# Mid and last chunks of a spectral mix: y of two more chunks spread by TensorE instead of by DMA, and three pieces of TensorE work moved

## The chip, the cores and the metric

The kernel runs on one core of a Trainium2 chip. The metric is the device time of one execution in microseconds (us). Times without a unit are us from the start of the profiled span.

## What is computed

The program is a causal attention with a cumulative bias, followed by a mix in the frequency domain:

```python
# q, k, v: (8, 8, 576, 64); s: (8, 8, 576); w_r, w_i: (64, 512, 512); w_ch: (512, 512)
scores = q @ k^T / sqrt(64) + min(-(cum[i] - cum[j]), 0), causal
x = softmax(scores) @ v                        # as (8, 576, 512)
X = rfft(x, axis=1)                            # along the sequence
Yr = Xr*w_r - Xi*w_i ; Yi = Xr*w_i + Xi*w_r    # 64 modes, each its own 512x512 pair
y = irfft(Y padded with zeros, n=576)
u = x + y
out = u + max(u @ w_ch, 0)                     # (8, 576, 512), float32
```

## The kernel before, in words

**Stages.** Attention goes over 32 steps (four groups g of two heads, eight batches b each). Its result x stays on chip as `x_all`. Per step a small product with sines and cosines gives the 64 modes of x, kept in `xs`. Group by group, the modes are multiplied by their weights: `modes(g, c)` (L430) takes chunk c of eight modes, with four weight tiles x = 0 to 3 (real and imaginary part, even and odd modes) of 512 KB each, and sixteen matmuls of 32 columns, four side by side in the column groups of the array. Groups 0 to 2 add up in `y_acc`; the last group's result plus `y_acc` goes to `yb` (L455, VectorE), which is Y of chunk c with 128 rows: four mode pairs, real and imaginary part, and batch.

**Weights.** 128 weight tiles, 64 MB in the type they have on chip, are streamed by GpSimd's queue (L217) into a ring of eleven slots (`wpool`) for the last 52 of them. A tile's transfer is issued when the matmuls that read the slot's former tile are done.

**The order of the work** is written out by hand (`manual_schedule`): each engine runs its instructions in program order, and waits on semaphores only for its data and for the release of tiles. The part that matters here is the loop over the eight chunks of the last group (L757 to L790) and what it calls:

- The final result of a row block is relu((x + y) Wch) + x + y. A "pair" is two row blocks of 128; there are 18. For 16 of them x Wch is made early and kept: six during attention, ten ("late") in this loop. `work()` (L673) does one step of that: `x_transposed` (L586: eight matmuls with the identity, two VectorE copies L596) of the next pair, and `keep` (L607) of the pair before: eight matmuls (L602), then ScalarE's copy (L492); for pairs of way "e" ScalarE's copy (L494) and VectorE's residual (L495). The calls go around the chunk loop by `TAKE` (L687) and by `gather`'s `turns`. The two first pairs' products, `x_times_wch(0)` and `(1)`, stay in PSUM.
- To add y, the inverse transform needs Y with modes on the partitions: tile `yv`, partition 16c + (8 modes, two parts), with batch, "which" (0 for y, 1 for v = y Wch) and 512 columns behind it. There are two ways to it. `spread` (L464) is a DMA transfer on SP's queue of 128 KB from `yb` or `vb` to `yv`. `gather` (L641) reads `yt_first`, kept transposes of y of several chunks, and picks one batch's columns as the stationary side; 64 columns at a time (two batches side by side) it makes v (moving side Wch, L653) and y (moving side the identity), and ScalarE (L665) and VectorE (L663) copy each to `yv`.
- Chunks 0 to 3: `y_transposed` (L622: four transposes, ScalarE's copy L627) into `yt_first`; after chunk 3, `gather(0, 4, 3)`: four blocks of v and y, with `work()` after the first three.
- Chunks 4 and 5: `modes` (it spreads y), `y_transposed` into a small tile, `y_times_wch` (L630: four matmuls L633, VectorE's copy L637, spread of v). After them the last `work()`, `x_transposed(0)`, `x_times_wch(0)`.
- Chunk 6: the same with the two first pairs' work between; chunk 7: `modes` with the first pairs' sums between its weight tiles (`first_u` ahead of x = 2, `first_z` ahead of x = 3). Y of chunks 6 and 7 is added straight from `yb` for the first two pairs (`add_last`), and spread for the others.
- Then, for the other pairs, the sums with x, y and the kept products, relu on ScalarE, the final add on VectorE and the output transfers on SP.

**PSUM.** `yp` (modes), `yt_ps`, `v_ps` and `yg_ps` share a ring of two banks, tag "aux" (L106); `xt_ps` a ring of two ("u"), `z_ps` a ring of two ("z").

Of the kernel before, what the change touches and what calls it, by code (L numbers as in the profile page):

```python
# [9 lines left out]
FP32 = mybir.dt.float32  # L10
FP16 = mybir.dt.float16
# [7 lines left out]
def kernel(  # L19
# [14 lines left out]
    DM = H * D  # L34
    P = 128
# [5 lines left out]
    DT = DM // P  # L41
# [5 lines left out]
    NCK = NM // MC  # L47
# [57 lines left out]
    spool = ctx.enter_context(tc.tile_pool(name="small_sb", bufs=2))  # L105
    auxpool = ctx.enter_context(tc.tile_pool(name="aux_psum", bufs=2, space=PSUM))  # L106
# [323 lines left out]
    def modes(g, c, meanwhile=None):  # L430


        ps = auxpool.tile([P, DM], FP32, name="yp", tag="aux")
        for x in range(4):
            ri, par = divmod(x, 2)
            cols = xs[g % 2].rearrange("p k r b m -> p (k r b) m")
            c0 = (48, 16)[ri] - 16 * par
            if meanwhile and x in meanwhile:
                meanwhile[x]()
            for cg in range(4):  # L440
                nc.tensor.matmul(  # L441
                    ps[32 * cg : 32 * cg + 32, :],
                    cols[:, c0 : c0 + 32, c * MC + 2 * cg + par],
                    wt[(g, c, ri, par)][:, cg, :],
                    start=(x == 0), stop=(x == 3),
                    tile_position=(0, 32 * cg), skip_group_check=True,
                )
        if g == 0:
            nc.vector.tensor_copy(out=y_acc[:, c, :], in_=ps)
        elif g < NG - 1:  # L450
            nc.vector.tensor_tensor(out=y_acc[:, c, :], in0=ps, in1=y_acc[:, c, :], op=ALU.add)
        else:
            yb = spool.tile([P, DM], FP16, name="y_sb", tag="y")
            for cols in halves if c == NCK - 1 else [slice(0, DM)]:
                nc.vector.tensor_tensor(  # L455
                    out=yb[:, cols], in0=ps[:, cols], in1=y_acc[:, c, cols], op=ALU.add
                )
            if c >= NCK // 2:
                spread(c, 0, yb)
            return yb  # L460

# [2 lines left out]
    def spread(c, which, rows):  # L464

        nc.sync.dma_start(out=yv[16 * c : 16 * c + 16, :, which, :], in_=rows)
# [113 lines left out]
    def parts(b, T):  # L580

        if T < NF:
            return [(slice(0, P), b, ident16h)]
        return [(slice(NL * i, NL * i + NL), b + i, ident16h[:NL, :NL]) for i in range(2)]

    def x_transposed(i):  # L586
        xts[i] = xt_sb[len(xts) % 2]
        for x, (b, T) in enumerate(pairs[i]):
            ps = upool.tile([P, DT, P], FP32, name="xt_ps", tag="u")
            for rows, bb, ident in parts(b, T):  # L590
                for dt in range(DT):
                    nc.tensor.matmul(
                        ps[:, dt, rows], x_all[: rows.stop - rows.start, dt, bb, T, :],
                        ident, start=True, stop=True, skip_group_check=True,
                    )
            nc.vector.tensor_copy(out=xts[i][:, x], in_=ps)  # L596

    def x_times_wch(i, last):
        zs[i] = z = zpool.tile([P, 2, DM], FP32, name="z_ps", tag="z")
        for x in range(2):  # L600
            for dt in range(DT):
                nc.tensor.matmul(  # L602
                    z[:, x, :], xts[i][:, x, dt, :], wch_sb[:, dt, :],
                    start=(dt == 0), stop=(last and dt == DT - 1), skip_group_check=True,
                )

    def keep(i):  # L607
        x_times_wch(i, True)
        j = late.index(i)
        if j < len(places):  # L610
            t = places[j]
        else:
            t = wpool.tile([P, WM, DM], BF16, name="z1", tag="w").rearrange("p m e -> p (m e)")
        kept_place(i, t)
        keep_product(i, slice(0, 2), zs[i])
# [3 lines left out]
    NY = NCK // 2  # L619
    yt_first = finpool.tile([P, DT, NY, P], FP16, name="yt_first")  # L620

    def y_transposed(yb, c=NCK):  # L622
        ps = auxpool.tile([P, DT, P], FP16, name="yt_ps", tag="aux")
        for dt in range(DT):
            nc.tensor.transpose(ps[:, dt, :], yb[:, bass.ts(dt, P)], ident16h)
        yt = yt_first[:, :, c, :] if c < NY else spool.tile([P, DT, P], FP16, name="yt_sb", tag="yt")
        nc.scalar.copy(out=yt, in_=ps)  # L627
        return yt

    def y_times_wch(c, yt):  # L630
        vp = auxpool.tile([P, DM], FP32, name="v_ps", tag="aux")
        for dt in range(DT):
            nc.tensor.matmul(  # L633
                vp, yt[:, dt, :], wch_sb[:, dt, :], start=(dt == 0), stop=(dt == DT - 1)
            )
        vb = spool.tile([P, DM], FP16, name="v_sb", tag="v")
        nc.vector.tensor_copy(out=vb, in_=vp)  # L637
        spread(c, 1, vb)
        return vb

    def gather(c0, c1, turns):  # L641

        n = 2 * MC * (c1 - c0)
        rows = slice(2 * MC * c0, 2 * MC * c1)
        ng = P // n
        for b0 in range(0, B, ng):
            vp = auxpool.tile([P, DM], FP32, name="v_ps", tag="aux")
            yp = auxpool.tile([P, DM], FP32, name="yg_ps", tag="aux")
            for which, ps in ((1, vp), (0, yp)):
                for dt in range(DT):  # L650
                    for g in range(ng):
                        op = yt_first[:, dt, : c1 - c0].rearrange("p c (x b) -> p (c x) b", b=B)
                        nc.tensor.matmul(  # L653
                            ps[n * g : n * g + n, :] if which else ps[n * g : n * g + n, bass.ts(dt, P)],
                            op[:, :, b0 + g],
                            wch_sb[:, dt, :] if which else ident16h,
                            start=(dt == 0 or not which), stop=(dt == DT - 1 or not which),
                            tile_position=(0, n * g), skip_group_check=True,
                        )
                for g in range(ng):  # L660
                    dst, src = yv[rows, b0 + g, which, :], ps[n * g : n * g + n, :]
                    if g % 2:
                        nc.vector.tensor_copy(out=dst, in_=src)  # L663
                    else:
                        nc.scalar.copy(out=dst, in_=src)  # L665
            if turns:
                turns -= 1
                work()


# [2 lines left out]
    def work():  # L673

        if not order_z and not ahead:
            return
        if order_z:
            i = order_z.pop(0)
            x_transposed(i)
            ahead.append(i)  # L680
        if len(ahead) == 2 or not order_z:
            i = ahead.pop(0)
            keep(i)

    late = [i for i in kept if i not in first_pairs]
    order_z = list(late)
    TAKE = (3, 2, 2, 0, 0, 0)  # L687
    us, rs = {}, {}
    GK = P - 2 * MC * NX

# [66 lines left out]
    for c in range(NCK - 2):  # L757
        yb = modes(NG - 1, c)
        for x in range(TAKE[c] - 1):
            work()  # L760
        yt = y_transposed(yb, c)
        if TAKE[c]:
            work()
        if c >= NY:
            y_times_wch(c, yt)
        elif c == NY - 1:
            gather(0, NY, 3)
    work()
    assert not order_z and not ahead
    c = NCK - 2  # L770
    x_transposed(0)
    x_times_wch(0, False)
    yb6 = modes(NG - 1, c)
    x_transposed(1)
    yt = y_transposed(yb6)
    x_times_wch(1, False)
    vb6 = y_times_wch(c, yt)
# [14 lines left out]
    yt = spool.tile([P, DT, P], FP16, name="yt_sb", tag="yt")  # L792
    for x in range(2):
        dts = slice(x * DT // 2, (x + 1) * DT // 2)
        ps = auxpool.tile([P, DT // 2, P], FP16, name="yt_ps", tag="aux")
# [5 lines left out]
    for cols in halves:  # L801
        vp = auxpool.tile([P, DM // 2], FP32, name="v_ps", tag="aux")
# [81 lines left out]
```

## Time and profile before

| | before |
|---|---|
| median of 6 runs | 458.14 us (456.3 to 458.77) |
| the profiled execution | 458.25 us, span 456.4 us |
| TensorE matmuls | 347.9 us busy (76%), 4201 |
| TensorE weight loads | 220.1 us busy (48%), 4233 |
| VectorE | 238.2 us busy (52%), 531 |
| ScalarE | 219.7 us busy (48%), 386 |
| GpSimd | 183.0 us busy (40%), 269 |
| mean granted TensorE clock | 0.872 |
| DMA | 94.01 MB, 206 GB/s over the span |
| the two spread kinds, `yv<-y_sb` and `yv<-v_sb` | 4 each, 128 KB each, 5.6 and 4.4 us to land (medians) |

How to read it: the page's 40 slices are 11.4 us each; a digit is the busy share in tenths, and for PEclk the clock granted to TensorE. A timeline line has start, duration, engine, line of the kernel, operation, out<-in, partitions and sizes, and how many instructions of that kind follow each other; in square brackets, how long the engine was idle before the first of them and what ended that. PE is TensorE, DVE VectorE, ACT ScalarE, POOL GpSimd, SP the queue of SyncE. The span goes from the first instruction to the last; the execution's time has 1.85 us around it.

### The profile page before, as it was taken

The page shows a single profiled execution, that of the slowest core. Times are in us where ns is not written, and L with a number is a line of the kernel's source. Part 1 is how long each engine was busy: PE and PEld are TensorE (multiplying, and loading weights), DVE is VectorE, ACT ScalarE, POOL GpSimd, SP SyncE. Part 2 cuts the span into 40 slices and gives each one's busy share as a digit, 9 for nine tenths or more (in the row PEclk, how much of TensorE's full clock was granted, in tenths as well). Part 3 has the DMA queues.
Part 4 walks back from the last instruction along what each step waited for, and adds up shares of the span by engine and source line. Part 5 has one row for each costly group of instructions (what it writes and reads, how often), then busy time and mean ns, then how long its engine had stood idle before and what let it go on. Part 6 is the DMA issues. An engine that isn't in the chain of part 4 may idle for free.

```text
span 456.4 us, 10298 instructions
## 1 busy us (share of the span) xinstructions
PE 347.9 (76%) x4201; PEld 220.1 (48%) x4233; DVE 238.2 (52%) x531; ACT 219.7 (48%) x386; POOL 183.0 (40%) x269
## 2 busy tenths in 40 slices
PE   1879888966562978826587778799879769689995
PEld 1456666644342656614455555466545336334432
DVE  7775665653242556614345535455745425532796
ACT  1585886554241657713445345366632224211774
POOL 6755555544345555334454454355423231300000
PEclk9997999997587899967778769799986978779999
DMA  9999999999999999999999999999999999993688
GB/s 178 201 203 203 202 201 204 203 204 204 204 204 201 202 203 203 203 205 204 200 196 204 204 204 205 203 203 202 207 206 208 206 207 206 210 217 76 226 297 318
DMA packets 108799, 94.01 MB, mean 206 GB/s; under 512 B 28416, under 2 KB 103936, under 8 KB 108752
## 3 DMA queue, kind: packets, MB, share of 16 engines
q0 software_dynamic: 98960, 81.81, 113.1%
q1 hardware_dynamic: 9792, 11.55, 8.0%
q8 instruction: 33, 0.54, 0.4%
q14 instruction: 14, 0.11, 0.1%
HBM read 164.56 MB, written 9.44 MB: 381 GB/s over the span
## 4 chain that ended last, share of the span: by engine, by line
DMA 55%; PE 28%; DVE 8%; issue 4%; POOL 2%; ACT 1%; SPq 0%; DVEq 0%; POOLq 0%; ACTq 0%
DMA w_sb<-in_moe_w_r_dram 20%; DMA w_sb<-in_moe_w_i_dram 17%; DMA q<-in_q_dram 13%; DMA k<-in_k_dram 4%; PE sc_ps L365 4%; PE av_ps L394 3%; PE yp L441 3%; PE sc_ps L359 3%; PE tr_ps L324 3%; PE z_ps L695 2%; DVE qtB L327 2%; PE ft_ps L418 2%; PE u_ps L714 1%; DVE qtA L327 1%; PE u_ps L695 1%
## 5 line engine op out<-in xcount | busy, mean ns | idle before, releaser
L373 ACT ACTIVATE p_sb<-sc_ps,cumt_sb 128x576 f16<-128x576 f32 (+1 forms) x256 | 141.9, 635 | 47.6 <-PE sc_ps L365 47.1
L217 POOL DMA_DIRECT2D w_sb<-in_moe_w_i_dram x60 | 45.1, 751 | 86.3 <-PE yp L441 42.0
L217 POOL DMA_DIRECT2D w_sb<-in_moe_w_r_dram x60 | 45.4, 757 | 62.6 <-DMA w_sb<-in_moe_w_r_dram 24.2
L217 POOL DMA_DIRECT2D v<-in_v_dram x72 | 50.8, 707 | 31.0 <-DMA v<-in_v_dram 8.4
L359 PE MATMUL sc_ps<-negm,ident 128*128 128x256 bf16 x256 | 56.4, 307 | 0.2
L324 PE MATMUL tr_ps<-ident,q 64*64 64x64 bf16 x576 | 17.4, 210 | 50.1 <-DMA q<-in_q_dram 50.0
L441 PE MATMUL yp<-w_sb,xs 128*32 128x512 bf16 x480 | 37.2, 417 | 16.7 <-DMA w_sb<-in_moe_w_i_dram 11.7
L327 DVE COPY qtA<-tr_ps 64x576 bf16<-64x576 bf16 x32 | 23.7, 742 | 46.0 <-PE tr_ps L324 46.0
L394 PE MATMUL av_ps<-v,p_sb 128*128 128x65 f16 x1024 | 45.4, 199 | 0.0
L344 ACT ACTIVATE p<-sc_ps,cumt 128x64 f16<-128x64 f32 x32 | 10.0, 313 | 71.5 <-PE sc_ps L340 71.5
L394 PEld LDWEIGHTS <-p_sb 128*128 128x128 f16 x1024 | 40.3, 101 | 5.0 <-issue 1.0
L327 DVE COPY ktA<-tr_ps 64x576 bf16<-64x576 bf16 x32 | 24.0, 749 | 33.0 <-PE tr_ps L324 33.0
L324 PEld LDWEIGHTS <-q 64*64 64x64 bf16 x576 | 13.6, 123 | 52.8 <-DMA q<-in_q_dram 51.7
L365 PE MATMUL sc_ps<-qtB,ktB 128*128 128x64 bf16 (+2 forms) x160 | 35.1, 325 | 3.7 <-issue 2.4
L365 PE MATMUL sc_ps<-qtA,ktA 65*128 65x512 bf16 (+2 forms) x192 | 37.4, 305 | 0.3 <-DVE ktA L327 0.3
L399 DVE TENSOR_REDUCE den<-av_ps 128x5 f32<-128x10 f32 x64 | 10.8, 169 | 51.1 <-PE av_ps L394 51.1
L441 PEld LDWEIGHTS <-xs 128*32 128x32 bf16 x512 | 22.5, 170 | 26.7 <-issue 23.3
L404 DVE TENSOR_TENSOR x_all<-av_ps,rcp 128x320 f16<-128x320 f32 x64 | 31.5, 492 | 2.2
L365 PEld LDWEIGHTS <-ktB 128*128 128x128 bf16 x192 | 22.5, 117 | 15.1 <-issue 6.6
L327 ACT COPY ktB<-tr_ps 64x576 bf16<-64x576 bf16 x32 | 20.3, 633 | 19.5 <-DVE ktA L327 18.5
L602 PE MATMUL z_ps<-wch_sb,xs 128*128 128x512 f16 x96 | 28.0, 444 | 0.8 <-DVE xs L596 0.8
L324 PE MATMUL tr_ps<-ident,k 64*64 64x64 bf16 x576 | 17.6, 211 | 13.8 <-DVE qtB L327 10.1
(117 smaller groups left out, 532.4 us busy)
## 6 DMA issues: line engine op xcount, KB each, us to landing
w_sb<-in_moe_w_r_dram POOLq DMA_DIRECT2D x60, 512.0 KB, 11.9
w_sb<-in_moe_w_i_dram POOLq DMA_DIRECT2D x60, 512.0 KB, 11.9
q<-in_q_dram POOLq DMA_DIRECT2D x32, 144.0 KB, 9.7
k<-in_k_dram POOLq DMA_DIRECT2D x32, 144.0 KB, 10.0
v<-in_v_dram POOLq DMA_DIRECT2D x72, 64.0 KB, 9.7
out_dram<-r_sb SPq DMA_DIRECT2D x16, 256.0 KB, 2.2
out_dram<-r_w SPq DMA_DIRECT2D x16, 256.0 KB, 2.7
x_all<-in_moe_w_i_dram POOLq DMA_DIRECT2D x3, 512.0 KB, 10.1
```

The lines of the kernel that those rows point to most:

```text
L217: nc.gpsimd.dma_start(out=dst, in_=src)
L324: nc.tensor.transpose(ps[rows, r, :], src[rows, r, :], ident16[rows, rows])
L327: copy(out=dst[n % NQ][rows, :].rearrange("d (p r) -> d p r", r=R), in_=ps[rows].rearrange("d r p -> d p r"),)
L359: nc.tensor.matmul(ps[:, bass.ds(w * S, W)], ident16, negm[:, bass.ts(r, W)], start=True, stop=False, skip_group_check=True,)
L365: nc.tensor.matmul(ps[:, c0 : c0 + i1 - i0], keys[:, w, r, :], qt[:, i0:i1], start=False, stop=True, skip_group_check=True,)
L373: nc.scalar.activation(out=pt[:, poff[x] : poff[x] + S - w * W], in_=ps[:, w * S : (w + 1) * S - w * W], func=ACTF.Exp, bias=cumt_sb[:, x, ...
L394: nc.tensor.matmul(ps[:, I, r : r + NCH], lhsT, rhs, start=(i == 0), stop=(i == len(todo) - 1), skip_group_check=True,)
L399: nc.vector.tensor_reduce(out=den, in_=ps[:, :, 0 : VW : NCH], axis=mybir.AxisListType.X, op=ALU.add)
L404: nc.vector.tensor_tensor(out=x_all[:, g, b, :, D * h : D * h + D], in0=ps[:, :, 1 : NCH], in1=rcp.unsqueeze(2).to_broadcast([P, NT, D]), ...
L441: nc.tensor.matmul(ps[32 * cg : 32 * cg + 32, :], cols[:, c0 : c0 + 32, c * MC + 2 * cg + par], wt[(g, c, ri, par)][:, cg, :], start=(x == ...
L602: nc.tensor.matmul(z[:, x, :], xts[i][:, x, dt, :], wch_sb[:, dt, :], start=(dt == 0), stop=(last and dt == DT - 1), skip_group_check=True,)
L695: nc.tensor.matmul(dst[x][r, :], G_sb[rows, bass.ds(T * P, r.stop - r.start)], yv[rows, bb, which, :], start=start, stop=True, skip_group_ ...
```

## The change

Four edits, all in the chunk loop of the last group:

1. y of chunks 4 and 5 is no longer spread by a transfer. Their transposes are kept in `yt_first` (slots 0 and 1, free after the first gather), and after chunk 5 a second `gather` makes y alone from them: 32 columns (two chunks of 16 rows) a matmul, four batches in the four column groups, two blocks of sixteen matmuls, four copies to `yv` a block. v of these chunks is spread as before.
2. `gather` takes a list of kinds, and allocates a bank for each as it comes to it.
3. `work()` in the first gather comes after its second and its fourth block, instead of after its first, second and third. One step of `work()` goes between `y_transposed` and `y_times_wch` of chunk 4, the last step to the same place of chunk 5.
4. `x_transposed(0)` goes between `modes` and `y_transposed` of chunk 5.

The number of the `work()` steps and the order of the pairs are the same.

```diff
-            if c >= NCK // 2:
+            if c >= NCK - 2:
                 spread(c, 0, yb)
...
-        yt = yt_first[:, :, c, :] if c < NY else spool.tile([P, DT, P], FP16, name="yt_sb", tag="yt")
+        yt = yt_first[:, :, c % NY, :] if c < NCK - 2 else spool.tile([P, DT, P], FP16, name="yt_sb", tag="yt")
...
-    def gather(c0, c1, turns):
+    def gather(c0, c1, turns, kinds):
...
-            vp = auxpool.tile([P, DM], FP32, name="v_ps", tag="aux")
-            yp = auxpool.tile([P, DM], FP32, name="yg_ps", tag="aux")
-            for which, ps in ((1, vp), (0, yp)):
+            for which in kinds:
+                ps = auxpool.tile([P, DM], FP32, name="g_ps", tag="aux")
...
-            if turns:
-                turns -= 1
+            if b0 // ng in turns:
                 work()
...
-    TAKE = (3, 2, 2, 0, 0, 0)
+    TAKE = (3, 2, 2, 0, 1, 1)
...
+        if c == NCK - 3:
+            x_transposed(0)
         yt = y_transposed(yb, c)
         if TAKE[c]:
             work()
         if c >= NY:
             y_times_wch(c, yt)
+            if c == NCK - 3:
+                gather(NY, NCK - 2, (), (0,))
         elif c == NY - 1:
-            gather(0, NY, 3)
-    work()
+            gather(0, NY, (1, 3), (1, 0))
     assert not order_z and not ahead
     c = NCK - 2
-    x_transposed(0)
     x_times_wch(0, False)
```

## The prediction

> All times are us of the profiled execution unless marked ns. Chunks are called by the code's c (0 to 7), so "chunks five and six" are c=4 and c=5.
>
> **What bounds the kernel now.** I read the page's slices first, then the chain of waits, the timelines of TensorE, VectorE and ScalarE from 366 to 423, and last busy time by stretches.
>
> ```profile
> PEclk9997999997587899967778769799986978779999
> DMA  9999999999999999999999999999999999993688
> ```
>
> DMA is full for 36 of 40 slices (to 410.7): the weight stream bounds the kernel until TensorE has chunk 3's last tile at 372.88. The diff touches nothing earlier. From there to 421.9 TensorE's own order decides; the stage after it (sixteen pairs of results) is carried by VectorE, 2.5 to 2.9 busy in most 3 us stretches from 432 on, and only shifts. So I follow TensorE to the last weight product (x=3 of c=7), which starts at 418.04. TensorE timeline:
>
> ```profile
> 375.41 1.99 PE L653 MATMUL v_ps<-wch_sb,yt_first 128*64 128x512 f16 x8 [0.67 <-ACT yt_first L627]
> ...
> 381.60 1.14 PE L653 MATMUL v_ps<-wch_sb,yt_first 128*64 128x512 f16 x8
> 382.57 0.58 PE L653 MATMUL yg_ps<-ident16h,yt_first 128*64 128x128 f16 x8
> 383.08 0.62 PE L592 MATMUL xt_ps<-ident16h,x_all 128*128 128x128 f16 x8
> 383.54 1.89 PE L602 MATMUL z_ps<-wch_sb,xs 128*128 128x512 f16 x8
> ...
> 392.27 1.12 PE L441 MATMUL yp<-w_sb,xs 128*32 128x512 bf16 x16 [1.60 <-DMA w_sb<-in_moe_w_r_dram]
> 394.19 0.40 PE L625 MATMUL yt_ps<-ident16h,y_sb 128*128 128x128 f16 x4 [0.80 <-DVE y_sb L455]
> 395.27 1.89 PE L633 MATMUL v_ps<-wch_sb,yt_sb 128*128 128x512 f16 x4 [0.68 <-ACT yt_sb L627]
> ```
>
> TensorE waits 1.60, 0.80 and 0.68 here, the last two again for c=5. The 1.60 is put down to a DMA, wrongly I think: that weight tile was issued at 355.52 and such tiles land 19.8 later. VectorE's timeline names another: the copy that frees the accumulator bank (ring of two, tag "aux") ends at 392.22, late because the residual of an "e" pair (L495) ran first.
>
> ```profile
> 390.27 1.22 DVE L495 TENSOR_TENSOR y_acc<-z_ps,y_acc 128x1024 f16<-128x1024 f32 x1 [0.50 <-ACT y_acc L494]
> 391.53 0.69 DVE L663 CAST yv<-v_ps 64x512 f16<-64x512 f32 x1
> ```
>
> Busy time by stretches (length, then busy and count of TensorE's matmuls, its weight loads, VectorE, ScalarE and GpSimd, then granted clock, DMA share, GB/s):
>
> ```profile
> 391.21:394.62 3.41, 1.52 (x20) 0.91 (x19) 2.28 (x4) 0.15 (x1) 1.48 (x2) 1.00 1.24 206
> 394.62:398.03 3.41, 2.76 (x16) 0.92 (x20) 0.69 (x1) 0.58 (x1) 1.49 (x2) 0.50 1.24 206
> 398.03:401.45 3.42, 1.93 (x17) 0.61 (x10) 0.69 (x1) 0.58 (x1) 0.74 (x1) 0.50 1.22 218
> 401.45:404.86 3.41, 3.41 (x9) 1.22 (x8) 0.69 (x1) 0.00 (x0) 0.00 (x0) 0.50 1.20 230
> 404.86:408.27 3.41, 2.85 (x20) 1.43 (x18) 1.29 (x2) 1.01 (x1) 0.00 (x0) 1.00 1.23 214
> ...
> 336.59:340.01 3.42, 2.02 (x32) 1.40 (x34) 1.45 (x6) 0.59 (x1) 1.25 (x2) 1.00 1.24 207
> ...
> 162.52:165.93 3.41, 1.71 (x30) 1.24 (x31) 1.68 (x3) 0.90 (x4) 1.44 (x2) 1.00 1.33 200
> ...
> 66.94:70.36 3.42, 2.14 (x36) 1.36 (x34) 1.92 (x3) 2.42 (x6) 1.59 (x3) 1.00 1.30 202
> ```
>
> All changes of the granted clock lie on one grid of 3.413. A stretch with 1.52 busy is followed by half clock; after 2.02 (336.59) the clock fell, after 1.71 and 2.14 it did not. From half clock it came back only after stretches at least 3.06 busy. So the waits cost twice: from 394.62 to 404.86 products take double (y times Wch 1.82 start to start against 0.96 at 412.82), some 3.7 in all.
>
> The Trainium skill, "TensorE: Matmul & The Clock Gate", Part 1, has the clock fall only after a whole idle window of about 3.4 us. The row of 391.21 contradicts it. By the rule the two falling-clock rivals below could not happen; by the row they can. The forecast's sum is one and the same.
>
> **The change, walked along TensorE.** Start-to-start costs at full clock: gather's v block 0.97, its y block 0.51, a pair's transposes 0.46, its product 1.82 before a switch to narrow tiles and 1.73 otherwise, the sixteen weight products 1.05 (408.57 to 409.62), transposes of y 0.24, y times Wch 0.96. At half clock: 1.78, 0.58, 0.83 and 427 ns a product matmul.
>
> Gather of c=0 to 3: two blocks now follow each other without a pair between. Block 0 is as before (375.41 to 377.77), but block 1's first bank is free only when ScalarE's and then VectorE's copy is through, 378.05+0.69=378.74: start 378.79, a gap of 1.02. It leaves the stretch from 377.55 with 2.5 busy instead of 3.42, too little to bring the clock back, so I keep half clock to 384.38 (before: 380.97). Block 1 ends 381.15, the pair's transposes 381.98, its product with 5.6 matmuls slow and 2.4 fast 385.0. Block 2 to 386.48; its bank comes free 2.48 after its start (381.60 to 384.08 in the rows), so block 3 starts 387.53, a gap of 1.05; then 389.01, and the second pair ends 391.29. The weight products of c=4 start there, 0.98 earlier, with one pair (2.2) fewer done; the 1.60 wait is gone since a pair now lies between.
>
> c=4: the wait for y_sb stays: 1.92 from the weight products to the transposes gives 393.21. Then the moved pair (2.19) covers the 0.68 wait, y times Wch starts 395.64, c=5's weight products 396.60, x_transposed(0) 397.65 to 398.11. What is late next is VectorE: the moved pair is the "e" one, and its residual now stands before v_sb(4) and y_sb(5). ScalarE L494 starts 1.93 after the product (395.84), VectorE L495 1.04 later (396.88), v_sb 1.26 after that (398.14), y_sb 0.61 on (398.75), the transposes 0.75 on: 399.50, a gap of 1.39 in place of 0.87.
>
> c=5: the last pair covers the 0.68 wait: 401.47; y times Wch to 402.43. Here the new gather comes: 32 matmuls of 32 columns by 128. No row has that form. The nearest are 64 ns each (eight yg_ps in 0.51) and 66 ns each (sixteen weight products in 1.05); four side by side in a quarter of the first would be 16 ns, half clock on the second 132. I take 64, the nearest in width: 2.05. At 16 the copies below would hold c=6 instead, and the sum falls by 1.0; at 132 it rises by 2.2. To 404.47; x_times_wch(0), its 0.56 wait gone, to 406.30.
>
> Evacuation of the new gather: eight copies of 32x512, four to a bank. Rows of 64 and 128 partitions both take VectorE 0.69, so I take 0.58 and 0.69. Ends are the 256-column row (0.42 each: y_sb(6) on time, 0.7 less) and the 576-column one (0.74 each: 0.7 more). VectorE's copy starts only when ScalarE's on the same bank has ended (377.44+0.58, then 378.05), so the four go in turn: start 403.65, then 404.26, 404.98, 405.59; the bank is free at 406.28 and c=6's weight products start 406.33. The second bank's chain ends with VectorE at 407.53, and y_sb(6) queues behind it at 408.14 instead of 407.44: transposes 408.89 (gap 1.05 against 0.41), x_times_wch(1) when xs is copied, 409.49 and 410.09, v to 412.18. Then as before: 2.02 to x=2 (414.20), 2.24 to x=3: **416.44 against 418.04, 1.60 less**.
>
> The Trainium skill, "TensorEngine Tiling", PSUM Bottleneck, warns that tiling does not speed evacuation and advises using both engines. Were they parallel, y_sb(6) would be on time and the sum 0.7 lower, 455.95; the serial rows speak against it.
>
> At nothing I cost the two y transfers removed (SP, 5.6 to land): their readers at 414.83 showed no wait, and 131 KB each at 208 GB/s frees 1.26 of the stream. That stream hides: its traffic ended near 415.0, so x=3's tile may come at 413.7, before 416.44; tiles 123 to 127 of the stream are issued when c=4's and c=5's first products free their slots, 0.98 and 0.49 earlier. SP keeps the order of the rest.
>
> Sum: span 456.4-1.60=454.8; with the 1.85 around it the execution is 458.25-1.60=456.65. The median before is 458.14, 0.11 under that execution.
>
> **Rivals.**
> - One clock fall. The stretch from 398.03 would hold the 1.39 gap and 2.06 busy, between the rows 2.02 (fell) and 2.14 (held). Then from 401.45 y times Wch costs 0.8 more, gather 0.3, product 0.2: 456.65+1.3=457.95. Against: 1.71 held at 162.52. The grid is not tied to the program, so each run may differ; runs before spread from 456.3 to 458.77.
> - Slower: two falls. The gap between blocks 2 and 3 leaves 2.36; if narrow matmuls count less than full ones there, 387.79 to 391.21 goes at half clock too, 1.65 more, and with the one above 459.6. It decides when a stretch with 2.3 busy of narrow products no longer holds the clock; for it speaks the fall after 2.02, against it 2.14 holding.
> - The weights bound. If the gaps come shorter (copies overlap, VectorE's residual slips behind y_sb), TensorE meets the last tile at 413.7 to 414: 4.2 less, 454.05.
> - The removed transfers bring the gain by themselves: nothing waits for them, so apart from the new order this part only adds its gather, 2.05. That is in the sum, and has no chance of its own.
>
> **Numbers.** Forecast 0.43, one fall 0.28, two falls 0.17, weights bound 0.12. About 0.3% (1.37) is what a measurement can tell from no change, so faster means under 456.77. The forecast lies only 0.12 below that; I give 0.35 of its 0.43 to faster and the rest to same. With the weights-bound case faster is 0.47, same 0.36, slower 0.17. The low end takes in the weights bound, 454.0; the high end, 459.2, leaves out only two falls and takes in the matmul form's and the copies' ends (+2.2, +0.7 from the forecast, one at a time). Cases of both signs hold much: the forecast's own range is 455.8 to 457.3.
>
> **What would show it.** Right: no 1.60 wait ahead of c=4; two gaps near 1.0 inside the gather, waiting on VectorE; half clock to 384.4 and none from 394 to 405; a gap of 1.4 ahead of c=5's transposes with L495 just before; y_sb(6) behind L662; x=3 near 416.4 without a DMA wait; the stage after unchanged at 38.4 from x=3 to the end of the span. Wrong: half clock after 401, the 32-column matmuls far from 64 ns, or x=3 waiting for its tile.

## The result, and the profile after

| | before | after |
|---|---|---|
| median | 457.92 us (46 runs, 456.03 to 459.91) | 455.79 us (21 runs, 455.14 to 457.64) |
| ratio of the times | | 0.996, 95% interval 0.995 to 0.997 |
| profiled execution, span | 458.25, 456.4 | 457.64, 455.9 |
| chunk 3's last weight product starts | 372.88 | 374.16 |
| the last weight product (x=3 of c=7) starts | 418.04 | 417.42 |
| from the one to the other | 45.16 | 43.26 |
| from there to VectorE's last group of adds | 32.69 | 32.68 |

The changed kernel is 0.4% faster; 1.6 us were forecast, 2.1 measured between the medians (1.8 by the ratio). The two profiled executions differ by less (457.64 is the slowest of the 21), because in this one chunk 3's last tile came 1.28 later; over all profiles of this study it came between 372.87 and 374.44, whatever was changed behind it. So the tail is best read from that tile on, in two lengths: to the last weight product ("the walk" below), and from there to VectorE's last adds, which is 32.7 in all profiles but one (experiment 8).

TensorE's timeline of the changed kernel (start, duration, engine, line, operation, count; in brackets the idle time before it and what ended it):

```profile
374.16 0.66 PE L441 MATMUL yp<-w_sb,xs 128*32 128x512 bf16 x4 [2.05 <-DMA w_sb<-in_moe_w_i_dram]
...
380.30 1.98 PE L652 MATMUL g_ps<-wch_sb,yt_first 128*64 128x512 f16 x8 [0.96 <-DVE yv L662]
...
389.15 1.14 PE L652 MATMUL g_ps<-wch_sb,yt_first 128*64 128x512 f16 x8 [0.99 <-DVE yv L662]
...
392.91 1.12 PE L441 MATMUL yp<-w_sb,xs 128*32 128x512 bf16 x16
394.83 0.40 PE L625 MATMUL yt_ps<-ident16h,y_sb 128*128 128x128 f16 x4 [0.80 <-DVE y_sb L455]
...
400.96 0.40 PE L625 MATMUL yt_ps<-ident16h,y_sb 128*128 128x128 f16 x4 [1.09 <-DVE y_sb L455]
...
403.88 0.48 PE L652 MATMUL g_ps<-ident16h,yt_first 128*32 128x128 f16 x16
404.73 0.48 PE L652 MATMUL g_ps<-ident16h,yt_first 128*32 128x128 f16 x16 [0.37 <-DVE v_sb L637]
405.14 1.90 PE L602 MATMUL z_ps<-wch_sb,xs 128*128 128x512 f16 x8
407.09 1.11 PE L441 MATMUL yp<-w_sb,xs 128*32 128x512 bf16 x16
...
409.87 0.40 PE L625 MATMUL yt_ps<-ident16h,y_sb 128*128 128x128 f16 x4 [1.11 <-DVE y_sb L455]
...
417.42 0.47 PE L441 MATMUL yp<-w_sb,xs 128*32 128x512 bf16 x4
```

The two new gaps inside the first gather are there (0.96, 0.99), the wait of 1.60 ahead of c=4 is gone, the gap ahead of c=5's transposes has grown from 0.81 to 1.09 and that of c=6 from 0.25 to 1.11, and the last product waits for no tile. From it to the end of the span are 38.45, against 38.41 before. VectorE ahead of c=5's transposes, and its last adds before and after:

```profile
398.48 1.22 DVE L495 TENSOR_TENSOR y_acc<-z_ps,y_acc 128x1024 f16<-128x1024 f32 x1 [1.71 <-ACT y_acc L494]
399.63 0.68 DVE L637 CAST v_sb<-v_ps 128x512 f16<-128x512 f32 x1
400.22 0.68 DVE L455 TENSOR_TENSOR y_sb<-yp,y_acc 128x512 f16<-128x512 f32 x1
```

```profile
450.73 2.48 DVE L748 TENSOR_TENSOR r_sb<-u_ps,r_sb 128x512 f32<-128x512 f32 x4
450.10 2.48 DVE L746 TENSOR_TENSOR r_sb<-u_ps,r_sb 128x512 f32<-128x512 f32 x4
```

Busy time by stretches, on the grid of this execution (TensorE's matmuls first, granted clock third from the end):

```profile
392.95:396.36 3.41, 2.61 (x33) 1.66 (x33) 2.17 (x5) 1.60 (x2) 2.49 (x4) 1.00 1.25 208
...
399.77:403.19 3.42, 2.33 (x16) 1.16 (x15) 2.33 (x4) 0.65 (x2) 0.00 (x0) 1.00 1.24 206
403.19:406.60 3.41, 3.04 (x43) 1.56 (x42) 1.64 (x3) 2.37 (x4) 0.00 (x0) 1.00 1.22 218
406.60:410.01 3.41, 2.25 (x30) 1.24 (x28) 2.71 (x5) 0.88 (x2) 0.00 (x0) 1.00 1.22 219
```

No stretch there is under 2.25 busy, and the clock stays at 1.00 from 386.12 on. Before, the stretch with 1.52 was followed by 10.24 at half clock. The same for the whole walk, before and after:

```profile
372.88:418.04 45.16, 38.10 (x259) 19.34 (x259) 17.62 (x26) 10.63 (x16) 6.67 (x9) 0.81 1.12 193
374.16:417.42 43.26, 36.21 (x290) 20.08 (x290) 20.09 (x30) 12.93 (x20) 6.67 (x9) 0.86 1.13 194
```

Length less busy time is TensorE's idle time: 7.06 before and 7.05 after. The waits that the new order covers and the gaps that it opens cancel, so the shorter walk is not idle time saved. Half clock lasted 17.07 before (6.83 and 10.24, TensorE busy for 14.3 of it) and 11.96 after (busy for 9.5). Work at half clock takes double, so the difference is worth some 2.4 (an estimate); the second gather adds work against it, and 1.9 is left.

### The profile page after: what moved, and what is told of

The parts are those of the page before. It is cut to its first block, busy times and chain, and to the rows that moved or that the text cites. A ratio compares the mean times of both kernels' runs of the same rounds, so it can differ in the third digit from the quotient of the medians.

```text
span 455.9 us, 10370 instructions
## 1 busy us (share of the span) xinstructions
PE 347.8 (76%) x4233; PEld 221.6 (49%) x4265; DVE 241.4 (53%) x535; ACT 222.2 (49%) x390; POOL 182.9 (40%) x269
## 4 chain that ended last, share of the span: by engine, by line
DMA 56%; PE 28%; DVE 6%; issue 4%; POOL 3%; ACT 2%; DVEq 0%; POOLq 0%; ACTq 0%
DMA w_sb<-in_moe_w_i_dram 29%; DMA q<-in_q_dram 12%; DMA w_sb<-in_moe_w_r_dram 10%; DMA k<-in_k_dram 4%; PE yp L441 3%; PE z_ps L602 3%; PE sc_ps L365 3%; PE av_ps L394 2%; PE tr_ps L324 2%; PE sc_ps L359 2%; PE z_ps L693 2%; PE g_ps L652 2%; PE u_ps L712 1%; PE ft_ps L418 1%; PE u_ps L693 1%
## 5 line engine op out<-in xcount | busy, mean ns | idle before, releaser
L394 PE MATMUL av_ps<-v,p_sb 128*128 128x65 f16 x1024 | 46.4, 201 | 0.0
L394 PEld LDWEIGHTS <-p_sb 128*128 128x128 f16 x1024 | 41.3, 103 | 5.3 <-issue 1.3
L365 PE MATMUL sc_ps<-qtA,ktA 65*128 65x512 bf16 (+2 forms) x192 | 39.4, 317 | 0.4 <-DMA qtA<-ncum_sb 0.4
L365 PE MATMUL sc_ps<-qtB,ktB 128*128 128x64 bf16 (+2 forms) x160 | 34.0, 317 | 3.5 <-issue 2.2
L365 PEld LDWEIGHTS <-ktB 128*128 128x128 bf16 x192 | 22.1, 115 | 14.3 <-issue 5.7
L365 PEld LDWEIGHTS <-ktA 65*128 65x128 bf16 x192 | 20.4, 107 | 13.0 <-issue 3.0
```

The lines of the kernel that those rows point to most:

```text
L365: nc.tensor.matmul(ps[:, c0 : c0 + i1 - i0], keys[:, w, r, :], qt[:, i0:i1], start=False, stop=True, skip_group_check=True,)
L394: nc.tensor.matmul(ps[:, I, r : r + NCH], lhsT, rhs, start=(i == 0), stop=(i == len(todo) - 1), skip_group_check=True,)
```

## The experiments

My theory after the result: TensorE's order sets the tail, the clock that it keeps is most of the gain, and the removed transfers are hidden. Rivals: the removed transfers are the gain; the covered waits are the gain and the clock is a side show; the weight stream's end is the real bound. Each was run beside the kernel before on the same chip; the chips differ from round to round, and the ratio is what compares across them (the median of before was 458.01 beside experiments 1 to 4, 457.84 beside 5 to 8 and 457.45 beside 9 to 11). In the table, "walk" is from chunk 3's last weight product to the last one, and "tile waits" what TensorE waited for tiles of c=6 and c=7 in it.

| kernel | median | ratio to before (95%) | walk | tile waits |
|---|---|---|---|---|
| before | 457.92 | | 45.16 | 0 |
| changed | 455.79 | 0.996 (0.995 to 0.997) | 43.26 | 0 |
| 1 order only | 457.68 | 0.9992 (0.9977 to 1.0007) | 43.41 | 2.26 |
| 2 gather only | 460.9 | 1.0072 (1.0047 to 1.0097) | 47.48 | 0 |
| 3 before, kept warm | 457.43 | 0.9997 (0.9981 to 1.0012) | 43.60 | 2.03 |
| 4 one engine a bank | 455.91 | 0.9958 (0.9943 to 0.9973) | 42.29 | 1.60 |
| 5 changed, short stream | 456.47 | 0.9963 (0.9949 to 0.9976) | 42.84 | 0 |
| 6 order only, short stream | 455.52 | 0.9952 (0.9936 to 0.9968) | 41.50 | 0.96 |
| 7 kept warm, short stream | 455.53 | 0.9952 (0.9934 to 0.9969) | 41.77 | 0 |
| 8 late spreads | 456.4 | 0.9976 (0.9963 to 0.9989) | 41.48 | 0.83 |
| 9 late spreads, v first | 455.26 | 0.9951 (0.9934 to 0.9968) | 41.92 | 0 |
| 10 transfers back | 457.08 | 0.9993 (0.998 to 1.0006) | 43.35 | 1.71 |
| 11 changed again | 456.25 | 0.9963 (0.9947 to 0.9979) | 42.24 | 0 |

A walk is that of one execution, and a kernel's own walks differ: 43.26 and 42.24 for the changed kernel. Chunk 3's last tile comes at 373.5 on average over the 13 profiles; with the walk, the 38.4 to 39.3 from the last product to the end of the span, and 1.85, this gives each kernel's median within 0.5. It does not for the profile of before (458.9 against 457.92) and the first one of the changed kernel (457.1 against 455.79). As an estimate, their usual walks are 44.2 and 42.0.

**1. Order only.** The changed kernel without its second gather:

```diff
-            if c >= NCK - 2:
+            if c >= NCK // 2:
                 spread(c, 0, yb)
...
-            if c == NCK - 3:
-                gather(NY, NCK - 2, (), (0,))
```

> The new order of the pairs and of x_transposed(0), but y of c=4 and c=5 goes by the spreading transfer as before; no second gather. Order theory (the gain comes from TensorE's order, the second gather costs): the gather's 1.26 us (403.88 to 405.14 in the changed kernel) goes, and y_sb(6) no longer queues behind its copies (about 0.9), so TensorE would reach the last weight product 2.1 earlier, 415.3 in that profile; the two transfers put 1.26 back on the weight stream, so the last tile may bound it at about 415 to 416. Expected median 453.7 to 454.6, faster than the changed kernel by 1.2 to 2.1. Transfer theory (the removed transfers bring the gain): the gain is gone, 457.5 to 458.5.

Measured 457.68, no gain that can be told from none. This is the number of the transfer theory, which experiment 2 contradicts; the order theory's number fails. TensorE did get earlier, and then stood still:

```profile
405.77 0.45 PE L441 MATMUL yp<-w_sb,xs 128*32 128x512 bf16 x4 [0.24 <-DMA w_sb<-in_moe_w_i_dram]
...
411.01 0.46 PE L441 MATMUL yp<-w_sb,xs 128*32 128x512 bf16 x4 [0.22 <-DMA w_sb<-in_moe_w_r_dram]
...
414.39 0.45 PE L441 MATMUL yp<-w_sb,xs 128*32 128x512 bf16 x4 [1.52 <-DMA w_sb<-in_moe_w_i_dram]
...
416.96 0.46 PE L441 MATMUL yp<-w_sb,xs 128*32 128x512 bf16 x4 [0.28 <-DMA w_sb<-in_moe_w_i_dram]
```

The products of x=2 and x=3 of c=7 wait longest for their tiles, 1.52 and 0.28. The walk less all four waits is 41.15, two less than the changed kernel's; the stream gives 43.41. This is a second bound, which my prediction had placed 2.7 ahead of TensorE.

**2. Gather only.** The kernel before with the second gather after chunk 5 (with the kept transposes and the list of kinds that it needs, edits 1 and 2), and nothing moved:

```diff
             y_times_wch(c, yt)
+            if c == NCK - 3:
+                gather(NY, NCK - 2, 0, (0,))
```

> The order of before, but y of c=4 and c=5 goes through kept transposes and a second gather after c=5. Order theory: slower than before by the second gather, 1.26 at full clock and up to about 2.2 where it falls into half clock (401.45 to 404.86 in the profile of before), with up to 0.5 for copies ahead of x_transposed(0)'s: 459.2 to 460.4. Transfer theory: at least as fast as the changed kernel's gain over before, 455.8 to 456.5.

460.9, slower than before by 0.7%: the transfer theory fails, and the order theory's range is missed by 0.5. The walk is 2.32 longer. Its timeline says three things at once:

```profile
393.67 1.12 PE L441 MATMUL yp<-w_sb,xs 128*32 128x512 bf16 x16 [1.60 <-DVE yv L662]
...
405.30 0.65 PE L652 MATMUL g_ps<-ident16h,yt_first 128*32 128x128 f16 x16 [0.20 <-DVE v_sb L637]
405.88 1.99 PE L602 MATMUL z_ps<-wch_sb,xs 128*128 128x512 f16 x8
...
410.62 1.90 PE L602 MATMUL z_ps<-wch_sb,xs 128*128 128x512 f16 x8 [2.30 <-DVE xs L596]
```

The 1.60 ahead of c=4 is here put down to VectorE's copy, as I had argued against the page of before. The gather itself is 1.4 (404.45 to 405.88) at half clock, which came back only at 406.10. And the copies hold up VectorE's copy of x_transposed(0): a wait of 2.30 where it was 0.56, 1.74 more where I had expected up to 0.5. So the transfers' removal alone is a loss, and the gather's price in this order lies more in VectorE's queue (1.74) than on TensorE (1.4).

**3. Before, kept warm.** Three matmuls whose result nobody reads, in each of the four waits of c=4 and c=5 (`warm(n)` multiplies the identity by a part of Wch n times into a bank of `xt_ps`'s ring):

```diff
+        if c >= NY:
+            warm(3)
         yt = y_transposed(yb, c)
+        if c >= NY:
+            warm(3)
```

> The kernel before with three extra matmuls (128x512, nobody reads their result) in each of the four waits of TensorE in c=4 and c=5, so that the waits stay as long but are not idle. Clock theory (most of the cost of those waits is the half clock that follows them): no half clock from 394 to 405, 3.7 less work time, bounded by the last tile near 415: 454.5 to 455.5. Cover theory (the gain is the covered waits themselves, the clock is a side show): no faster than before, 457.6 to 458.6, since nothing useful is moved into the waits.

457.43, and again neither as expected. TensorE's part came out as the clock theory has it: without tile waits the walk is 43.60-2.03=41.57, 3.6 less than before, though not one wait is covered with useful work. The stretch that had 1.52 busy and cost the clock:

```profile
391.00:394.40 3.40, 2.23 (x24) 1.23 (x24) 2.34 (x4) 0.22 (x1) 1.48 (x2) 1.00 1.24 206
394.40:397.80 3.40, 3.37 (x27) 1.27 (x24) 1.23 (x2) 0.59 (x1) 2.23 (x3) 1.00 1.24 206
```

On this execution's own grid the stretch is 390.87 to 394.28, with 2.11 busy, and the clock held. But the time did not follow, since x=2 and x=3 of c=7 wait 1.30 and 0.73 for tiles.

**4. One engine a bank.** The second gather's copies: the first bank's four on ScalarE, the second's on VectorE.

```diff
-                    if g % 2:
+                    if (b0 // ng if c0 else g) % 2:
```

> The changed kernel, with the second gather's copies dealt by bank (ScalarE takes the four of the first bank, VectorE the four of the second) instead of in turn within a bank. If the serial chain of copies is what delays y_sb(6) (409.12, after a last L662 at 408.39): VectorE's four start near 405.4 and end near 407.9, y_sb(6) starts right after c=6's weight products at about 408.1, 1.0 earlier, and the end moves by that, 454.8. If the gap ahead of c=6's transposes has another cause, no change: 455.6 to 456.0.

The serial chain was the cause of the gap ahead of c=6's transposes. VectorE in the changed kernel, then in this one:

```profile
405.01 0.69 DVE L662 CAST yv<-g_ps 32x512 f16<-32x512 f32 x1 [0.33 <-ACT yv L664]
406.33 1.41 DVE L662 CAST yv<-g_ps 32x512 f16<-32x512 f32 x2 [0.64 <-ACT yv L664]
408.39 0.69 DVE L662 CAST yv<-g_ps 32x512 f16<-32x512 f32 x1 [0.64 <-ACT yv L664]
409.12 0.69 DVE L455 TENSOR_TENSOR y_sb<-yp,y_acc 128x512 f16<-128x512 f32 x1
```

```profile
403.63 2.79 DVE L662 CAST yv<-g_ps 32x512 f16<-32x512 f32 x4 [0.57 <-PE g_ps L652]
406.52 0.69 DVE L455 TENSOR_TENSOR y_sb<-yp,y_acc 128x512 f16<-128x512 f32 x1
```

y_sb(6) starts 1.17 after c=6's weight products (405.35) instead of 2.03, and the gap falls from 1.11 to 0.25. The time stays, 455.91: TensorE now waits 1.23 and 0.37 for the last two tiles. Its bound, 42.29, is 1.1 to 1.3 lower than in experiments 1 and 3, the two kernels that have the transfers.

**5, 6, 7. Short stream.** The changed kernel, experiment 1 and experiment 3, each without the transfers of the last two weight tiles, to take the stream's end away:

```diff
+            if (g, c, ri) == (NG - 1, NCK - 1, 1):
+                wt[key] = wt[g, c, 0, par]
+                continue
             i = ring_of(len(wt))
```

> The changed kernel without the transfers of the last two weight tiles: the two imaginary tiles of c=7 are not loaded, and its products read the two real ones again (so those eight matmuls use the wrong weights). The stream ends some 5 us earlier, and only TensorE's order is left to bound the tail. If the changed kernel is bound by TensorE there, as its profile says (no wait on a tile up to 417.42): 455.4 to 456.2, no change. If in most runs the last tile binds it: 453.5 to 455.

> The new order with y of c=4 and c=5 spread by transfer (the first experiment), without the transfers of the last two weight tiles, whose products read the two real tiles of c=7 again. Stream theory (the order alone gained nothing since its TensorE met the last tiles, 2.26 of waits in its profile): those waits go, 1.8 to 2.4 off its 457.68: 455.3 to 455.9, or less if the end of the stream also slowed the output; against the changed kernel's TensorE it is up to 2 shorter, 453.8 to 454.6 if the stage behind follows in full. If the order alone has no gain for another reason: 457.2 to 458.

> The kernel before with the twelve extra matmuls in its waits, without the transfers of the last two weight tiles (products read the two real ones again). Clock theory with the stream as the bound: 3.6 of TensorE time that the clock gives back appears in full, 454.0 to 455.0, against 457.43 with the whole stream. If keeping the clock up is worth nothing: 457 to 458.

The changed kernel does not get faster (0.9963 against 0.996; its 456.47 is 0.3 above what I expected): in it TensorE's walk ends last, if by little. Orders 1 and 3 do, by 0.40% and 0.45% of before, 1.8 and 2.1 us: what they had won on TensorE was hidden behind the stream and comes out when it is shortened. In 6 a wait of 0.96 is left, for a tile of c=6; 7 is 0.5 above its expectation, though its walk is as expected. With 7, keeping the clock up is worth 3.4 of walk against the one profile of before (45.16 to 41.77) and 0.5% of the time, 2.2 us, and TensorE's work has grown by nothing but twelve idle matmuls. The kernel before alone with the short stream was not run; it waits for no tile there, so little is to be expected of it.

**8 and 9. Late spreads.** On top of experiment 4, the two transfers of c=6, which nobody reads before the results of the third pair, are issued after the stream; in 8 ahead of v of c=7, in 9 in the order of their readers (the edit of 9):

```diff
...
+    spread(NCK - 2, 1, vb6)
     spread(NCK - 1, 1, vb)
+    spread(NCK - 2, 0, yb6)
```

> The changed kernel with the second gather's copies dealt by bank, and the two spreading transfers of c=6 (131 KB each) issued only after c=7's y, when the weight stream is through. Stream theory: TensorE had 1.6 of waits on the last tiles with the copies by bank; 262 KB at 208 GB/s is 1.26 off the stream's end, and TensorE follows: 454.4 to 454.9, about 1.0 under the changed kernel. If the stream's end does not bind: 455.6 to 456.1, or later than that if the four transfers now land too late for the pairs behind (their first reader comes some 5 after the issue).

> Copies by bank as in the fourth experiment, and c=6's two spreading transfers after the weight stream, but now in the order of their readers: y of c=7, v of c=6, v of c=7, y of c=6. Stream theory: from chunk 3's last tile to the last weight product about 41.5 as with the late transfers before (42.3 without), and the wait of 0.7 on v of c=7 goes down to 0.2 or less, so that the stage behind is 32.7 to 32.9 long again: 455.2 to 455.6, the fastest. If the late transfers still hold up the readers: 456 to 456.5.

In 8 the last tile came earlier as expected (walk 41.48 against 42.29), but the gain was given back at the first reader of v of c=7, which was now the last of four in SP's queue:

```profile
422.48 0.60 PE L694 MATMUL z_ps<-yv,G_sb 128*128 128x512 f16 x2 [0.68 <-DMA yv<-v_sb]
```

The stage behind the last weight product was 33.52 instead of 32.7. In 9 that wait is gone (32.67), no tile is waited for, and 455.26 against 456.25 for the changed kernel on the same chip (seven runs from 454.92 to 456.37, and twelve from 455.89 to 457.18) make it the fastest of the kernels that use the right weights, 0.5% under before; six of its seven runs lie under all twelve. The walk, 41.92, is 0.4 longer than expected, and TensorE sets it.

**10. Transfers back.** Experiment 4 with the two y transfers of c=4 and c=5 added again, into rows that c=6 and c=7 write later. TensorE's program is the same.

```diff
-            if c >= NCK - 2:
-                spread(c, 0, yb)
+            if c >= NCK // 2:
+                spread(c + 2 if c < NCK - 2 else c, 0, yb)
```

> Copies by bank as in the fourth experiment, with the two y transfers of c=4 and c=5 put back on top of the second gather, into rows of yv that c=6 and c=7 write later (so they carry nothing that is used). TensorE's work and order are unchanged. Stream theory (262 KB under the stream's end move the last tile by about 1.2): from chunk 3's last tile to the last weight product 43.4 to 43.6 instead of 42.3, waiting on a tile, and 456.8 to 457.3 against 455.9. At-nothing theory (my prediction's step, the transfers are hidden): 455.6 to 456.1.

457.08, as the stream theory had it; by the ratios, which compare across chips, 0.35% of before or 1.6 us more than experiment 4:

```profile
410.46 0.69 PE L441 MATMUL yp<-w_sb,xs 128*32 128x512 bf16 x8
413.91 0.46 PE L441 MATMUL yp<-w_sb,xs 128*32 128x512 bf16 x4 [1.36 <-DMA w_sb<-in_moe_w_i_dram]
416.56 0.46 PE L441 MATMUL yp<-w_sb,xs 128*32 128x512 bf16 x4 [0.35 <-DMA w_sb<-in_moe_w_i_dram]
```

262 KB move the last tile by 1.06 in the walk (43.35 against 42.29), close to the 1.26 worked out from 208 GB/s. This is the step that my prediction had put at nothing. All profiles with the whole stream line up by what lies under it (landing of the last tile after chunk 3's last weight product, from its issue and its time to landing):

| transfers under the stream | kernels | last tile |
|---|---|---|
| v of c=4 and c=5 | 8, 9, nearly so 2 | 41.4 to 41.5 |
| also y and v of c=6 | changed, 4, 11 | 42.1 to 42.7 |
| also y of c=4 and c=5 | 1, 3, 10 | 43.3 to 43.6 |

In the kernel before, whose v of c=6 goes out only at 414.61, it is 42.7.

**11. Changed again,** beside 9 and 10: no edit.

> The changed kernel once more, on the same chip as the two others, for the comparison: 455.4 to 456.2; TensorE bound, no wait on a tile of c=7, 42.8 to 43.3 from chunk 3's last tile to the last weight product.

456.25, walk 42.24 without tile waits, 0.6 under what I expected: the last tile lands 0.1 before the last product starts in this execution, and 0.5 before it in the first profile (416.9 against 417.42). TensorE and the stream end close together.

## Why the prediction was right, and where it was not

- *The 1.60 wait is a bank, not a DMA.* Right: experiments 2 and 3 show it with VectorE as the releaser, and it is gone after.
- *Two gaps of 1.02 and 1.05 in the gather, half clock one stretch longer.* Right: 0.96 and 0.99 of idle, half clock to 386.12, 11.96 after chunk 3's last product (11.5 forecast). From chunk 3's last product to c=4's first 18.75 against 18.41 forecast. The length of half clock is not fixed by the program, though: with the same program up to c=4 it ended 9.9 after that product in experiment 11 and 8.9 in experiment 4, and c=4 came after 17.72 and 17.04.
- *No fall of the clock from 394 to 405.* Right, in every kernel with the new order and in experiment 3; both kernels with the old order and idle waits fell for 10.24. Experiment 7 has this gain without covering a wait, and the idle time of 7.06 and 7.05 shows that in the changed kernel too the clock is the gain on TensorE. The stretch I had feared, 399.77 here with 2.33 busy, held.
- *The "e" pair's residual delays y_sb(5).* Right: L495 runs from 398.48, y_sb(5) at 400.22; start to start the gap is 1.25 (1.39 forecast).
- *The new gather is 2.05 on TensorE, at 64 ns a matmul.* The size was off, and this was one of the prediction's own signs of being wrong: 16 matmuls in 0.41, 26 ns each, and 1.26 in all with a wait of 0.37 for a bank. The row of 64 columns was the wrong neighbour. The Trainium skill, "TensorE: Matmul & The Clock Gate", section LDWEIGHTS, has a weight load take columns / 1.2 ns; that makes, as an estimate, 53 ns for 64 columns and 27 for 32, beside 64 and 26 ns measured a matmul. That these matmuls cost what their loads do is likely, but no run here tests it.
- *y_sb(6) queues behind the serial copies.* Right: 409.12 after L662 at 408.39; experiment 4 removes it.
- *The sum.* Walk 43.56 forecast (416.44-372.88), 43.26 measured, and 42.24 in the second profile. Part of the nearness is luck, since errors cancel: against the forecast, the way to c=4 was 0.34 longer, from there to the second gather 0.17 shorter, from the gather to c=6's weight products 0.69 shorter, and the rest 0.22 longer. All that the second profile is shorter by lies ahead of c=4.
- *At nothing: the two transfers, with the stream's last tile at 413.7.* Wrong, and the step that failed. With TensorE as early as the new order makes it, the last tile comes 42.1 to 42.7 after chunk 3's, and 43.3 to 43.6 with the transfers; the forecast had 40.8 (413.7-372.88). With them TensorE waits for the stream, and no gain can be measured (experiments 1 and 10: 0.1%); without them it is 0.4%. Two readings were off. The last tile of before landed at 415.6, not near 415.0. And I had read it from a kernel in which TensorE was late; when TensorE is earlier, c=6's spreads are issued earlier too and fall under the stream (y of c=6 went out at 410.46 before, at 407.24 in experiment 4). Experiment 8 shows the size: these two moved away are worth 0.8 in the walk.

So the forecast's time was right by TensorE's side alone, and the list of causes lacked one: the order gives TensorE the gain, as clock, and the gather is the price for letting the stream keep up. Neither part alone gains anything that can be measured, and one alone loses. Whether the gather is needed stays open: the order alone with c=6's two transfers issued late was not run, and by the figures here its stream would end near 42.6 (43.4 less 0.8, an estimate), about where the changed kernel's does.

## What to carry to other kernels

Where an engine's order and a saturated stream end close together, a change has to move both: work out the walk of each from the last event they share, and see which ends last after the change, with all that the earlier engine now issues earlier. Short idle waits close together can cost more in TensorE's clock than in themselves (experiment 3: 3.6 of walk for four waits of 0.7 to 0.8 that stay as long); filling them even with idle matmuls shows what they cost. Before paying for the removal of transfers, see whether they can be issued after the stream, in the order of their readers, as experiment 9 did for c=6's two.

## What was not expected of the hardware

- Small SBUF to SBUF transfers through SP's queue are not free under a saturated stream: 262 KB moved its last tile by 1.06 (experiment 10 against 4) and 0.81 (experiment 8 against 4).
- One narrow matmul of 32 columns by 128, four column groups in turn, takes 26 ns, that of 64 columns 64 ns, for the same 128 columns of moving data.
- The granted clock fell after 3.41 us stretches that were partly busy, and not only after idle ones: 1.52 busy in the tail of before, 2.02 at 336.59. No one busy time decides it: 2.21 was followed by half clock in experiment 4 (250.07), while 1.67 (362.23) and 2.01 (164.26) held in the changed kernel, as did 2.33 and 2.25 in its tail. From half clock it came back after 3.06 or more before, after 2.91 at 119.88 in the changed kernel.
